# A retention and Fourier-mixing kernel on one core: every engine's queue behind the first batch put in an order that the program text computes

## The chip, the cores and the metric

The kernel runs on one core of a Trainium2 chip. A core has five engines, each with an instruction queue of its own that is worked off in order: TensorE (PE, matrix products; its weight loads are a second row, PEld), VectorE (DVE), ScalarE (ACT), GpSimd (POOL) and SyncE (SP), which here issues DMAs. Engines wait for one another by semaphores. The metric is the device time of one execution in microseconds (us), lower being better. The span is the part of it between the first and the last profiled instruction.

## What is computed

For 4 batches, 8 heads, 768 positions and 64 columns a head, a decaying state is run over the positions; the output (4 x 768 x 512) goes through a two-dimensional Fourier transform of which the real part is added, then through a normalization and two dense layers:

```python
gamma = 1.0 - 2.0 ** (-5.0 - np.arange(H))
for t in range(S):
    state = gamma[None, :, None, None] * state + np.einsum('bhd,bhe->bhde', k[:, :, t], v[:, :, t])
    y[:, :, t] = scale * np.einsum('bhd,bhde->bhe', q[:, :, t], state)
...
X = np.fft.fft(np.fft.fft(x, axis=1), axis=2)
u = x + np.real(X)
un = (u - mu) / np.sqrt(var + 1e-06)
return u + np.maximum(un @ w_ch1, 0.0) @ w_ch2
```

## The kernel before

**Stages of a batch.** Positions are cut into six chunks of 128. Heads are taken in four pairs. For a pair, q, k and v are loaded (`load_unit`, L159, three DMAs of 384 KB on SP's queue into tiles `in32`, 11 buffers), cast to half precision on POOL (`cast_unit`, L355: q16z, kd, v16) and q and k transposed (`t_unit`, L536: on PE with copies on ACT for batches 0 and 1, by DMA transposes on SP's queue for batches 2 and 3). Then come the products within a chunk (`a_unit`, wkA, masked by DVE into atm), the states (`kv_unit`, wkK, chained on DVE through s), and the outputs (`y_unit`, wkY, scaled by ACT into x). DVE folds x by the symmetries of the transform (`fold_s`, `fold_d`, `fold_e`), PE multiplies by cosine and sine tables along the positions (`s1_unit`) and along the columns (`s2_unit`, pq). There DVE makes u, POOL adds x to it (L864, L866), DVE takes mean and variance (bst, L883), and ACT writes the centred un (L885). `unT_unit` transposes un, by PE in batch 0 and half of batch 1, else by a DMA on SP's queue (L910). The dense layers follow for two halves of a batch: `h_unit` (`h0_unit` in the first half of batch 0) makes psh, which ACT or DVE turns into ht (L934, L936, or L954, L956), and `ch_unit` sums psc over 16 blocks of ht (L973), which DVE turns into ob (L977) for a store on SP's queue (L981).

**What runs over what.** The dense layers of batch b are PE's long work. Between their units the program puts the mixing of batch b's second half, and the loads, attention and first mixing of batch b+1. `emit` (L1086) does it: each stream of units gets a start and an end in units of a batch, its units are spread evenly between, and all are written in the order of these times. `dm`, `ts` and `da` (L1122 to L1142) are the starts and ends.

**What sets the order.** The program is written in that order, and the framework then orders each engine's queue with a cost model of its own, earlier text first among what it believes ready. The kernel holds this back in some places by edges that carry no semaphore. `pin` (L98) chains the instructions of the first batch's attention (`first_units`) on each engine, and later on those of POOL for all units with a time below 1.0; `behind` (L113) keeps the units below 1.0 behind the first batch; `held` (L121) and `issue_after` keep casts in turn and the eight maskp instructions (L232) behind one of ACT's. Loads also wait, with semaphores, for a weight load and a matmul (batch 1) or for a matmul of the batch before (batches 2 and 3): L161 and L166.

PSUM tiles, which PE writes and ACT or DVE frees, are of two tags: `g` with five buffers (pq, wkA, wkK, tq, most wkY) and `pm` with three (psh, psc, and the wkY of batch 0).

Of the kernel before, what the change touches and what calls it, by code (L numbers as in the profile page):

```python
# [11 lines left out]
AF = mybir.ActivationFunctionType  # L12
# [18 lines left out]
ON_ACT = {'q': (0, 1, 0), 'kv': (1, 1, 1), 'g': (0, 1, 1), 'gr': (0, 0, 0)}  # L31
FB = 1
NPE = 2
ACT_ROWS = ((2, 5, 6, 7, 8, 9, 10, 14), (0, 3, 6, 7, 9, 10, 11, 12, 14, 15), (2, 4, 5, 6, 7, 8, 10, 14))


@with_exitstack
def kernel(
# [55 lines left out]

    tails, base = {}, {}
    mark = [0]

    def pin(engines=None):  # L98
        ins = tc.nc.cur_bb.bb.instructions
        for n in range(mark[0], len(ins)):  # L100
            x = ins[n]
            e = str(x.engine)
            if engines is not None and not any(g in e for g in engines):
                continue
            if e in tails:
                tc.add_manual_dep(x, tails[e],
                                  mybir.DependencyInfo(mybir.DependencyClass.NoSync,
                                                       mybir.DependencyReason.DATA),
                                  reason="pinned order")
            tails[e] = x.name  # L110
        mark[0] = len(ins)

    def behind():  # L113
        for x in tc.nc.cur_bb.bb.instructions[mark[0]:]:
            if str(x.engine) in base:
                tc.add_manual_dep(x, base[str(x.engine)],
                                  mybir.DependencyInfo(mybir.DependencyClass.NoSync,
                                                       mybir.DependencyReason.DATA),
                                  reason="behind the first batch")

    def held(unit):  # L121
        def run():
            ins = tc.nc.cur_bb.bb.instructions
            n0 = len(ins)
            unit()
            for n in range(n0, len(ins)):
                m = n - 1
                while m >= 0 and ins[m].engine != ins[n].engine:
                    m -= 1
                if m >= 0:  # L130
                    tc.add_manual_dep(ins[n], ins[m].name,
                                      mybir.DependencyInfo(mybir.DependencyClass.NoSync,
                                                           mybir.DependencyReason.DATA),
                                      reason="casts in turn")
        return run


# [14 lines left out]
    def load_unit(b, i, after=None):  # L152
        def run():
            h0 = 2 * PAIR_ORDER[i]
            for name, src in srcs.items():
                t = inp.tile([P, 2, NCH, D], f32, tag="in32", name=f"{name}32")
                rows = "h (p c) d -> p h c d" if b < NPE and name == "q" else \
                    "h (c p) d -> p h c d"
                dma = nc.sync.dma_start(t, src[b, h0:h0 + 2].rearrange(rows, p=P))  # L159
                if after is not None:  # L160
                    for x in (w_dma[after].ins, lb[0]["mm"].ins):  # L161
                        tc.add_manual_dep(dma.ins, x.name,
                                          mybir.DependencyInfo(mybir.DependencyClass.Sync,
                                                               mybir.DependencyReason.DATA),
                                          reason="loads in turn")
                if b > 1:  # L166
                    tc.add_manual_dep(dma.ins, a_of[b - 1, 1].ins.name,
                                      mybir.DependencyInfo(mybir.DependencyClass.Sync,
                                                           mybir.DependencyReason.DATA),
                                      reason="loads behind the transposes")  # L170
                in_of[name, b, i] = t
        return run
# [56 lines left out]
    def late_consts():  # L229
        with tc.issue_after(lb[0]["una"].ins):  # L230
            for h in range(H):
                nc.scalar.activation(maskp[:, h // 2, h % 2], maskf, AF.Copy, bias=0.0,  # L232
                                     scale=float(gam[h] ** (-P)))

# [117 lines left out]

    at, q16_of, kd_of, v16_of, last_cast = {}, {}, {}, {}, {}

    def cast_unit(b, i):  # L355
        def run():
# [3 lines left out]
            v16 = vp.tile([P, NCH, 2, D], f16, tag="v16", name="v16")  # L360
            with ExitStack() as es:
                if b < NPE:
                    if (b, i - 1) in last_cast:
                        es.enter_context(tc.issue_after(last_cast[b, i - 1].ins))
                    q16 = qzs[i % 2].rearrange("p h c d -> p (h c d)")[
                        :, 0:NCH * P].rearrange("p (c h d) -> p c h d", c=NCH, h=2)
                    es.enter_context(tc.issue_after(nc.gpsimd.tensor_scalar(
                        out=q16, in0=q32.rearrange("p h c d -> p c h d"), scalar1=1.0,
                        scalar2=1.0, op0=ALU.mult, op1=ALU.mult).ins))
                else:  # L370
                    q16 = qzs[i % 2]
                    for h2 in range(2):
                        dst = q16[:, h2, :, D * h2:D * h2 + D]
                        nc.gpsimd.tensor_scalar(out=dst, in0=q32[:, h2], scalar1=1.0,
                                                scalar2=1.0, op0=ALU.mult, op1=ALU.mult)
                for h2 in range(2):
                    kc = nc.gpsimd.tensor_scalar(out=kd[:, :, h2, :], in0=k32[:, h2],  # L377
                                                 scalar1=gkd[:, h0 + h2:h0 + h2 + 1],
                                                 scalar2=1.0, op0=ALU.mult, op1=ALU.mult)
                    if b < NPE:  # L380
                        es.enter_context(tc.issue_after(kc.ins))
                last_cast[b, i] = nc.gpsimd.tensor_scalar(  # L382
                    out=v16, in0=v32.rearrange("p h c d -> p c h d"), scalar1=1.0, scalar2=1.0,
                    op0=ALU.mult, op1=ALU.mult)
            q16_of[b, i], kd_of[b, i], v16_of[b, i] = q16, kd, v16
# [26 lines left out]
    def v0_unit(i):  # L412
        def run():
            v32 = in_of.pop(("v", 0, i)).rearrange("p h c d -> p c h d")
            v16 = v16_of[0, i] = vp.tile([P, NCH, 2, D], f16, tag="v16", name="v16")
            n = NCH if i < 3 else 3
            last_cast[0, i] = nc.gpsimd.tensor_scalar(
                out=v16[:, 0:n], in0=v32[:, 0:n], scalar1=1.0, scalar2=1.0, op0=ALU.mult,
# [581 lines left out]
    def attn_steps(b):  # L1000
        steps = []
        for step in range(6):
            un = []
            if step < 4:
                un.append(held(cast_unit(b, step)))
            i = step - 1
# [79 lines left out]
    def emit(streams):  # L1086
# [5 lines left out]
        for e in ev:  # L1092
            e[3]()
            if e[0] < 1.0:
                behind()
                pin(None if e[0] < 0.05 else ["Pool", "GpSimd"])

    pin()
    for u in first_units():
        u()  # L1100
        pin()
    base.update(tails)
    first.close()
# [3 lines left out]
    for b in range(B):  # L1107
# [13 lines left out]
        s2s, unTs = mix_units(b, [3, 4, 5])  # L1121
        dm = (0.12, 0.24, 0.3, 0.38) if b == 0 else (0.004, 0.140, 0.232, 0.341)  # L1122
        streams += [(majors, b, b + 1.0), (s2s, b + dm[0], b + dm[1]),
                    (unTs, b + dm[2], b + dm[3])]
        if b + 1 < B:
            steps = attn_steps(b + 1)
            if b == 0:
                streams.append(([load_unit(1, i, 6) for i in range(4)], 0.180, 0.220))
                streams.append(([qt_zeros], 0.1, 0.15))
                streams.append(([half_tables], 0.655, 0.655 + 0.02))  # L1130
                streams.append(([pad_unit], 0.673, 0.703))
                ts = (0.249, 0.368, 0.410, 0.415, 0.507, 0.615, 0.680, 0.685)
            else:
                streams.append(([load_unit(b + 1, i) for i in range(4)], b + -0.370, b + 0.075))
                n = [len(u) for u in steps[1:]]
                ts = [-0.040, -0.020] + [0.050 + 0.585 * sum(n[:j]) / sum(n)
                                         for j in range(6)]
            streams.append((steps[0], b + ts[0], b + ts[1]))
            streams += [(u, b + ts[j + 2], b + ts[j + 3]) for j, u in enumerate(steps[1:])]
            end = b + ts[-1]  # L1140
            da = (0.062, 0.080, 0.173, 0.203, 0.271, 0.321) if b == 0 else \
                (0.063, 0.067, 0.048, 0.158, 0.168, 0.189)  # L1142
            streams.append(([s1_unit(b + 1, e, cb) for cb in range(2) for e in range(2)
                             if cb or b + 1 >= FB], end + da[0], end + da[1]))
            s2s, unTs = mix_units(b + 1, [0, 1, 2])
            streams += [(s2s, end + da[2], end + da[3]), (unTs, end + da[4], end + da[5])]
    emit(streams)


# [28 lines left out]
```

## Time and profile before

| | |
|---|---|
| median of 4 runs | 247.71 us (247.35 to 247.93) |
| the profiled execution | 247.35 us |
| its span | 245.4 us |
| matmuls, and other instructions busy | 2024; DVE 430, ACT 276, POOL 146 |
| dense layers, psc at L973 | 400 matmuls, busy 89.6 us |
| dense layers, psh at L930 | 448 matmuls, busy 81.3 us |
| moved by DMA | 36.39 MB, mean 148 GB/s |

A row of the profile's groups names the line, the engine, the operation, the tiles (out<-in), the shapes and the count, then the busy time, the mean of one and the idle time of its engine just before it with what ended that. The chain that ended last is followed backwards from the last instruction, at each step to what released it. In the 40 slices a digit is the busy share in tenths. "issue" is time in which an engine waited for nothing that the profile shows.

### The profile page before, as it was taken

How to read it: one execution, taken by the hardware profiler on the slowest of the kernel's cores; microseconds unless marked ns; L12 is line 12 of the kernel's file. 1: busy time of each engine (PE TensorE's matmuls, PEld its weight loads, DVE VectorE, ACT ScalarE, POOL GpSimd, SP SyncE). 2: the span in 40 equal slices, each digit the busy share in tenths (PEclk: the TensorE clock that was granted, in tenths of full speed). 3: DMA queues.
4: the chain of work that ended last, by engine and by line, in shares of the span. 5: the costliest groups of instructions: out<-in, count | busy, mean ns of one | idle time of the engine just before them, and what ended most of it. 6: DMA issues, size and time to landing. Idle time of an engine off the chain costs nothing.

```text
span 245.4 us, 5309 instructions
## 1 busy us (share of the span) xinstructions
PE 233.5 (95%) x2024; PEld 144.1 (59%) x2024; DVE 177.7 (72%) x430; ACT 124.1 (51%) x276; POOL 81.0 (33%) x146
## 2 busy tenths in 40 slices
PE   6797899999999999999999999999999998999994
PEld 2454668856776655665567446665676455445543
DVE  8999957899788788995986648887885657324112
ACT  8798678487786445742247416722357217202500
POOL 7667500494500068680001637650003214000000
DMA  8999999899999188989999489596100331121012
GB/s 177 259 258 145 202 198 198 185 250 265 279 218 227 26 171 189 196 165 148 262 277 203 97 177 188 103 137 161 47 0 3 63 130 33 35 85 43 0 45 85
DMA packets 99209, 36.39 MB, mean 148 GB/s; under 512 B 89840, under 2 KB 96240, under 8 KB 99184
## 3 DMA queue, kind: packets, MB, share of 16 engines
q1 hardware_dynamic: 94960, 31.86, 62.9%
q0 software_dynamic: 4224, 4.19, 10.7%
q8 instruction: 16, 0.26, 0.5%
q14 instruction: 9, 0.07, 0.1%
HBM read 27.26 MB, written 6.29 MB: 137 GB/s over the span
## 4 chain that ended last, share of the span: by engine, by line
PE 71%; DVE 9%; POOL 6%; ACT 5%; SPq 3%; DMA 2%; issue 2%; POOLq 0%; DVEq 0%
PE psc L973 30%; PE psh L930 23%; PE ps L730 3%; SPq L159 3%; PE psh L947 3%; PE wkA L594 3%; DMA k<-in_k_dram 2%; PE wkY L648 2%; DVE bst L883 2%; POOL u L866 2%; PE wkY L644 1%; POOL u L864 1%; PE wkK L613 1%; DVE u L834 1%; PE pq L827 1%
## 5 line engine op out<-in xcount | busy, mean ns | idle before, releaser
L973 PE MATMUL psc<-w,ht 128*128 128x512 f16 (+1 forms) x400 | 89.6, 370 | 0.1
L930 PE MATMUL psh<-unT,w 128*128 128x384 f16 x448 | 81.3, 326 | 0.6 <-ACT ht L934 0.6
L973 PEld LDWEIGHTS <-ht 128*128 128x128 f16 x400 | 38.1, 98 | 35.5 <-issue 0.3
L930 PEld LDWEIGHTS <-w 128*128 128x128 f16 x448 | 42.3, 98 | 24.9 <-issue 1.3
L934 ACT ACTIVATE ht<-psh 128x384 f16<-128x384 f32 x64 | 30.6, 488 | 39.4 <-PE psh L930 38.2
L864 POOL TENSOR_TENSOR u<-u,x 128x256 f32<-128x256 f32 x21 | 13.3, 635 | 102.6 <-DVE u L834 91.0
L977 DVE SCALAR_TENSOR_TENSOR ob<-psc,stats,u 128x512 f32<-128x512 f32 (+1 forms) x25 | 18.1, 722 | 27.1 <-PE psc L973 27.0
L936 DVE TENSOR_SCALAR ht<-psh 128x384 f16<-128x384 f32 x48 | 26.3, 549 | 8.6 <-PE psh L930 8.3
L597 DVE TENSOR_TENSOR atm<-wkA,maskp 128x512 f16<-128x512 f32 x36 | 23.9, 683 | 1.0 <-PE wkA L594 1.0
L885 ACT ACTIVATE un<-u,stats 128x512 f16<-128x512 f32 x21 | 15.1, 721 | 16.9 <-DVE stats L884 8.7
L883 DVE BATCH_NORM_STATS2 bst<-u 128x6 f32<-128x512 f32 x21 | 14.6, 694 | 9.8 <-POOL u L866 9.5
L623 DVE SCALAR_TENSOR_TENSOR s<-s,gk,wkK 128x128 f16<-128x128 f16 x48 | 16.4, 342 | 2.3 <-ACT s L619 1.4
L656 ACT ACTIVATE x<-wkY,gexp 128x384 f16<-128x384 f32 x24 | 12.8, 580 | 9.3 <-PE wkY L648 9.3
L145 PE MATMUL wps<-ht 128*128 128x512 f16 x40 | 12.6, 418 | 2.2 <-POOL ht L196 2.2
L377 POOL TENSOR_SCALAR kd<-k,gexp 128x384 f16<-128x384 f32 x24 | 13.9, 587 | 1.9 <-DMA k<-in_k_dram 1.9
L866 POOL TENSOR_TENSOR u<-u,x 128x256 f32<-128x256 f32 x21 | 13.3, 635 | 2.8 <-DVE u L858 1.3
L594 PE MATMUL wkA<-qTz,kT 128*128 128x256 f16 x72 | 13.6, 273 | 0.0
L829 ACT COPY qn<-pq 128x128 f32<-128x128 f32 x18 | 4.9, 274 | 14.1 <-PE pq L827 13.9
L947 PE MATMUL psh<-unT,w 128*128 128x128 f16 x192 | 11.5, 219 | 0.1
L947 PEld LDWEIGHTS <-w 128*128 128x128 f16 x192 | 11.0, 98 | 0.7 <-issue 0.5
L382 POOL TENSOR_SCALAR v<-v 128x768 f16<-128x768 f32 x12 | 10.0, 830 | 2.2 <-DMA v<-in_v_dram 2.1
L594 PEld LDWEIGHTS <-kT 128*128 128x128 f16 x72 | 6.9, 98 | 6.0 <-DVE s L623 0.4
(164 smaller groups left out, 317.3 us busy)
## 6 DMA issues: line engine op xcount, KB each, us to landing
q<-in_q_dram SPq DMA_DIRECT2D x16, 384.0 KB, 6.1
k<-in_k_dram SPq DMA_DIRECT2D x16, 384.0 KB, 5.6
v<-in_v_dram SPq DMA_DIRECT2D x16, 384.0 KB, 6.5
out_dram<-ob SPq DMA_DIRECT2D x23, 256.0 KB, 2.6
w<-in_moe_w_ch_dram POOLq DMA_DIRECT2D x8, 512.0 KB, 10.8
out_dram<-ob SPq DMA_DIRECT2D x2, 128.0 KB, 1.7
unT<-un SPq DMA_TRANSPOSE x15, 2.4
qTz<-q16z SPq DMA_TRANSPOSE x8, 3.8
```

What stands on the lines that cost most here:

```text
L594: mm = nc.tensor.matmul(wk[:, c2], st["kT"][:, c, :], st["qT"][:, :, c, :], start=True, stop=True)
L597: nc.vector.tensor_tensor(out=st["atm"][:, 2 * part:2 * part + 2], in0=wk, in1=maskp[:, PAIR_ORDER[i]].unsqueeze(1).to_broadcast([P, 2, 2, ...
L623: nc.vector.scalar_tensor_tensor(out=s16[:, c], in0=s16[:, c - 1], scalar=gk2[:, hp:hp + 1], in1=wk[:, c - c0], op0=ALU.mult, op1=ALU.add)
L864: nc.gpsimd.tensor_tensor(out=u[:, kb, 0:256], in0=u[:, kb, 0:256], in1=x[:, kb, 0, 1:257], op=ALU.add)
L866: nc.gpsimd.tensor_tensor(out=u[:, kb, 256:512], in0=u[:, kb, 256:512], in1=x[:, kb, 1, 257:1:-1], op=ALU.add)
L883: nc.vector.bn_stats(bst, u[:, kb, :])
L930: nc.tensor.matmul(psh, w116[:, cb, fb * P:(fb + 1) * P], unT[:, cb, rt * 384:(rt + 1) * 384], start=(cb == 0), stop=(cb == 3))
L934: nc.scalar.activation(ht16[:, fb, :], psh, AF.Relu, bias=0.0, scale=-1.0)
L936: nc.vector.tensor_scalar(out=ht16[:, fb, :], in0=psh, scalar1=-1.0, scalar2=0.0, op0=ALU.mult, op1=ALU.max)
L947: mm = nc.tensor.matmul(psh[:, f], w116[:, cb, fb * P:(fb + 1) * P], unT[:, cb, kb * P:(kb + 1) * P], start=(cb == 0), stop=(cb == 3))
L973: nc.tensor.matmul(psc[:, c0:c1], ht16[:, fb, rb3 * P:(rb3 + 1) * P], w216[:, fb, c0:c1], start=(fb == 0), stop=(fb == NFB - 1))
L977: nc.vector.scalar_tensor_tensor(out=ob[:, c0:c1], in0=psc[:, c0:c1], scalar=lb[b]["st"][:, rb, 3:4], in1=lb[b]["u"][:, rb, c0:c1], op0=AL ...
```

## The change

The helpers `pin`, `behind`, `held` and the uses of `issue_after` go. `emit` only writes units in the order of their times. All instructions written up to the end of `first_units` are counted as `kept`. At the end the new `order_queues` looks at every instruction, works out what each needs (tiles read and written, buffers of a ring, PSUM banks, the `told` semaphore edges of the loads), gives each a due time, plays the program through with durations from `instr_cost`, and chains each engine's instructions, SP's among them, in the order that results. Those in `kept` stay in program order.

A due time is worked out backwards. A PE instruction is due at the sum of the PE durations before it in the program. Any other is due 12 us after the PE time at its place in the program, or earlier, where something that needs it is due earlier, less its own duration and a lag. In the play-through each engine takes, among what is ready, what is due first. DMAs of SP share one ring (`dma`), POOL's another (`soft`).

```diff
+SLACK = 12000.0
+BY_DUE = ('PE', 'DVE', 'Activation', 'Pool', 'SP')
+def instr_cost(x, PSUM=PSUM):
...
+    if eng == "PE":
+        return max(n / 2.4 + 2.5, 27.0) * (0.5 if half else 1.0), n / 2.4 + 165.0
+    if kind == "InstDMACopy":
+        return (780.0 if eng == "Pool" else 400.0), None
+    if kind == "InstDmaTransposeAnt":
+        return 1400.0, 3800.0 if el > 600 else 2450.0
...
+            t = 100.0 + el * (1.04 if wide or not x.ins else 0.45)
+        return t, t + 80.0
+    if eng == "Activation":
+        t = 65.0 + 0.83 * el + (80.0 if scaled else 0.0) + (0.0 if psum else 90.0)
+        return t, t + 105.0
+    two = kind == "InstTensorTensor"
+    t = 80.0 + 2.3 * el if two else (250.0 + 0.7 * el if el > 300 else 80.0 + 1.0 * el)
+    return t, t + 30.0
+def order_queues(tc, told, kept):
...
+    for n in range(kept):
+        if eng[n] in last:
+            need[n][last[eng[n]]] = 0
+        last[eng[n]] = n
...
+    lag = {"DVE": 35.0, "Activation": 36.0, "Pool": 78.0, "PE": 79.0, "SP": 26.0}
...
+        due[n] = now + (0.0 if eng[n] == "PE" else SLACK)
+        if eng[n] == "PE":
+            now += spans[n][0]
+    for n in sorted(range(len(ins)), key=lambda n: -n):
+        for m, k in then[n]:
+            gap = 0.0 if not k or eng[n] == eng[m] == "PE" else lag[eng[m]] + (
+                spans[n][1] or 6000.0)
+            due[n] = min(due[n], due[m] - gap)
...
+        n = heapq.heappop(ready[e])[1]
+        order[e].append(n)
+        free[e] = t + busy
+        if span is None or e == "SP":
...
+                if not there:
+                    big = size > 600 * 128
+                    end = max(t + (3100.0 if big else 2500.0),
+                              dma + (1450.0 if big else 900.0))
+                    free[e] = max(t + 1220.0, end - 2400.0)
+                else:
+                    run = list(there[0].ap)[-1][1] * 4
+                    work = 4.0 * size / (217.0 if run <= 256 else 345.0)
+                    put = any(x is there[0] for x in list(ins[n].outs))
+                    end = max(t + 1500.0 + work + (0.0 if put else 700.0), dma + work)
+                    free[e] = max(t + (330.0 if put else 450.0),
+                                  end - (3000.0 if put else 4550.0))
+                dma = end
...
+    for v in order.values():
+        for a, b in zip(v, v[1:]):
+            tc.add_manual_dep(ins[b], ins[a].name,
+                              mybir.DependencyInfo(mybir.DependencyClass.NoSync,
+                                                   mybir.DependencyReason.DATA),
+                              reason="order of the queue")
...
-            if e[0] < 1.0:
-                behind()
-                pin(None if e[0] < 0.05 else ["Pool", "GpSimd"])
...
-        dm = (0.12, 0.24, 0.3, 0.38) if b == 0 else (0.004, 0.140, 0.232, 0.341)
+        dm = DM0 if b == 0 else DM1
...
     emit(streams)
+    order_queues(tc, told, kept)
```

The starts and ends become constants at the top of the file, and some have new values:

```diff
+DM0, DM1 = (0.120, 0.245, 0.307, 0.391), (0.054, 0.205, 0.240, 0.286)
+TS0 = (0.249, 0.336, 0.337, 0.405, 0.476, 0.584, 0.649, 0.654)
-                ts = (0.249, 0.368, 0.410, 0.415, 0.507, 0.615, 0.680, 0.685)
+TS1 = (-0.040, -0.020, 0.050, 0.585)
+DA0, DA1 = (0.069, 0.096, 0.179, 0.265, 0.276, 0.326), (0.063, 0.067, 0.048, 0.158, 0.168, 0.189)
-            da = (0.062, 0.080, 0.173, 0.203, 0.271, 0.321) if b == 0 else \
-                (0.063, 0.067, 0.048, 0.158, 0.168, 0.189)
+LD0, LD1 = (0.180, 0.220), (-0.370, 0.094)
-                streams.append(([load_unit(b + 1, i) for i in range(4)], b + -0.370, b + 0.075))
+HT0 = (0.655, 0.712, 0.673, 0.708)
-                streams.append(([half_tables], 0.655, 0.655 + 0.02))
-                streams.append(([pad_unit], 0.673, 0.703))
```

TS1, LD0 and DA1 hold the old values. No arithmetic and no shape of an instruction changes, and no instruction is added or taken away.

## The prediction

> **What bounds the kernel now.** I read the page first, its busy shares and its 40 slices.
>
> ```profile
> span 245.4 us, 5309 instructions
> PE 233.5 (95%) x2024; PEld 144.1 (59%) x2024; DVE 177.7 (72%) x430; ACT 124.1 (51%) x276; POOL 81.0 (33%) x146
> ...
> PE   6797899999999999999999999999999998999994
> ```
>
> TensorE (PE) is busy in nearly every slice after the sixth. So this isn't a kernel in which a queue order can uncover much: what it can give back is PE's own stops. The busy table by stage, then, to see where they are (columns: stretch, its length, busy time and instructions of PE, PEld, DVE, ACT, POOL, granted clock, DMA share, GB/s):
>
> ```profile
> 34.30:41.00 6.70, 6.43 (x93) 5.45 (x91) 4.20 (x12) 6.09 (x21) 0.26 (x4) 1.00 1.22 193
> ...
> 90.00:96.00 6.00, 5.48 (x45) 3.20 (x44) 4.85 (x13) 3.25 (x9) 4.64 (x9) 1.00 0.81 170
> 96.00:150.00 54.00, 54.00 (x428) 32.88 (x426) 41.51 (x98) 22.99 (x53) 19.32 (x33) 1.00 1.01 188
> 150.00:158.00 8.00, 7.60 (x74) 5.06 (x72) 7.09 (x18) 5.62 (x15) 6.15 (x12) 1.00 0.74 171
> ...
> 199.00:211.00 12.00, 11.28 (x76) 6.81 (x75) 9.27 (x22) 6.83 (x18) 3.68 (x6) 1.00 0.17 45
> ```
>
> The reader sees that the clock is full everywhere, and that PE's losses sit in a few short stretches (90 to 96, 150 to 158, 199 to 211). Over 34.3 to 242.3 us, which is what the change orders anew, these rows and the others of the table add up to 2.2 us of idle PE.
>
> That is too little by the end of each pipe: a lone 512-column matmul shows 379 ns, while 48 in a row take 10.36 us, 216 ns each, so every stop hides 163 ns more. I therefore took, in the trace, every distance from one matmul's start to the next one's and subtracted the usual step of its shape (216 ns for 512 columns, 162 for 384, 109 for 256, 56 for 128). From 34.2 us to the last matmul 202.1 us are such steps and **5.6 us** are excess. Eighteen stops of over 80 ns hold 4.9 of it. No order can gain more than 5.6, since the steps themselves stay.
>
> Here the Trainium skill ("Perfetto Trace Analysis", Identifying the Most-Contended Engine) warns that busy matmuls say little about headroom and that weight-load time is the better measure. The row for that is 59%, which read as headroom would be 41% of the span, 100 us. I go by the steps: one load here serves 384 or 512 streamed columns, so 59% cannot grow to 100 by reordering.
>
> **Which work stops PE.** Three pieces of the chain that ended last, for the largest stops:
>
> ```profile
> 90.98 0.62 POOL u L866
> 91.59 0.96 POOL q16z L374 x2
> 92.55 1.13 POOL kd L377 x2
> 93.68 0.81 POOL v L382
> 94.53 0.44 PE wkK L613 x5
> ```
>
> Batch 2's first casts stand behind the additions to u, though their loads had landed by 73.5 us (issued 64.9 to 66.3); PE waits at the wkK matmuls. The two stops there cost 0.84 us of excess, the twin at 155.8 to 156.7 (wkY waiting for DVE's u and atm) 0.73.
>
> ```profile
> 203.74 0.72 ACT L885 ACTIVATE un<-u,stats 128x512 f16<-128x512 f32 x1 [0.60 <-DVE stats L884]
> 204.37 1.23 ACT L934 ACTIVATE ht<-psh 128x384 f16<-128x384 f32 x3
> ...
> 206.29 0.72 ACT L885 ACTIVATE un<-u,stats 128x512 f16<-128x512 f32 x1 [0.36 <-issue]
> 206.92 0.85 ACT L934 ACTIVATE ht<-psh 128x384 f16<-128x384 f32 x2
> ```
>
> In the last batch ACT takes un, which feeds matmuls at 221.4, ahead of ht, for which PE already stands. The three stops from 204.4 to 210.6 are 0.365 + 0.600 + 0.240 = 1.21 us.
>
> ```profile
> 38.34 1.69 ACT L232 ACTIVATE maskp<-maskf 128x128 f32<-128x128 f32 x8
> 39.94 1.05 ACT L954 ACTIVATE ht<-psh 128x512 f16<-128x512 f32 x2
> ```
>
> ACT makes maskp (first used by atm at 57.7 us), and DVE clears qTz (two memsets of 378 ns), before the ht that frees PE's buffer: 0.28 us.
>
> **The change part by part.** *Removed*: the pins, `behind`, `held`, `issue_after`. They are edges without semaphores; no instruction goes, so 0. *Added*: one edge between each pair of neighbours on each queue, again no instruction and no semaphore, 0; the same 5309 instructions run. Should an edge make one more wait per stop, the nearest row is the 0.02 to 0.07 us of "issue" in the chain; over 18 stops 0.4 to 1.3 us, my upper bound on the loss; below, 0. I take 0. *The first batch* (`kept`) stays in order, so 0 to 34.3 us is unchanged, and so is the end: after the last matmul at 242.2 only ob (0.48) and its store follow.
>
> *The order itself.* An instruction of another engine is now due when the matmul that needs it is due, less its time. Un due at 221 goes behind ht due in a microsecond; maskp and the memsets, used over 12 us later, go behind ht; the casts run in POOL's own gap of 20 us before 86.7. So I take as gone the three big groups, 0.84 + 0.73 + 1.21 = 2.78, and 0.28 at 40.2: **3.06 us**. Cover of the moved work: un then has 211 to 221.4, where ACT and DVE are busy 0.00 and 1.95 of 10.40; without that cover it costs its old price, 1.2. POOL, once early with the casts, must still not be late with u, which stops nothing today but bst.
>
> I take as not gained the stops where the engines are full or the data late: 0.39 at 58 to 59 (two ACT copies of 0.79 and one of 0.80 in a row; DVE is at 16.4 of 19.0 from 41 to 60), 0.25 at 75 to 77 behind atm, 0.32 at 80.8 behind xg, 0.18 at 127 and 180, 0.65 at 34 to 38 behind the first batch's chain, and 0.8 in small ones. Were they all gone too, the gain would be 5.6; that is the low end.
>
> *What the model misjudges comes back as new stops*, since the order is fixed. Its cast of 384 elements takes 250 + 0.7 x 384 = 519 ns against 585 for kd, of 768 elements 788 against 831, its atm 632 against 681. Per pair of heads 2 x 66 + 43 + 3 x 49 = 0.32 us, for 12 pairs 3.9 us if nothing hides it, 0 if PE always has other work. PE had none for 5.6 of 208 us, so I lean to the low side and take 0.5 us (an estimate). *The new constants* (DM1 moves s2 of batches 1 to 3 from 0.004..0.140 to 0.054..0.205 of a batch, TS0 the casts of batch 1 from 0.368 to 0.336) change program order, hence the due times, those of the s2 by 0.05 to 0.065 of the 52 us between two batches, 2.6 to 3.4 us; the unT that they lead to are needed at half a batch, 26 us in. I take 0, as they move inside that; if the cover were gone, the price is the old one of such a stop, 0.6.
>
> *The SP queue* now carries loads, stores and transposes by due time. Each load holds the ring for 1.66 us (batch 1's twelve land between 47.46 and 65.75 us, 1.1 to 2.3 apart). The transposes must land before wkA: the cover from the later landing of a pair's two to its first wkA is 2.4, 0.6, 1.5, 2.1 us in batch 2 and 2.1, 2.9, 0.6, 3.6 in batch 3. So one load put ahead of every pair costs 1.06 + 0.16 + 1.06 = 2.3, none costs 0. Behind a transpose that waits on SP stand the next loads and the stores; ob has three buffers, so DVE's ob and then psc on PE would be late next. I take 0: the model bills ring time for loads (98,304 x 4 / 217 = 1.81 us) close to these rows, and today's order already puts a load of 6.6 us ahead of a transpose of 6.5 us without a stop. The Trainium skill ("DMA: Bandwidth & Descriptors", Anatomy of one DMA) has 2.0 us plus bytes over 436 GB/s for a transfer that GpSimd issues, which makes, as an estimate, 2.9 us for 384 KB and 0.9 of ring; the rows of this case's SP loads say 5.6 to 6.5 to landing. By the page a load ahead of every pair would cost only 0.3 + 0.3 = 0.6, and a model that bills twice its ring time would hold back transposes for nothing.
>
> **Sum**: 3.06 - 0.5 = 2.5 us. The profiled execution took 247.35 (span 245.4 and 1.95 around it); it was the fastest of four with median 247.71. 247.7 - 2.5 = **245.2**.
>
> **Rivals.** *Everything gained* (0.15): all stops but the first batch's 0.65 go, 5.0 less 0.3: 243.0. For it: every stop has work behind it that could go first. Against: DVE is at 7.09 of 8.00 from 150 to 158. *Moved, not removed* (0.10): PE, freed at 94 and 156, stands at the next fixed head; the 3.9 us of misjudged casts come in at three quarters and the sum is 0: 247.7. For it: stops with "issue" or atm as their end follow where PE runs ahead; against: misses of 0.05 us each are shorter than any stop counted. *Slower: transposes behind loads* (0.18). If due times put two loads (3.3 us) ahead of a pair, it overshoots its cover by 0.9, 2.7, 1.8, 1.2, 1.2, 0.4, 2.7, 0, mean 1.36; in three pairs of eight that is 4.1, less the 2.5 gained: 249.3. It decides from two pairs on. For it: batch 3's loads go out amid batch 2's transposes (96 to 118 us), both on SP. Against: the covers held with mixed orders so far. If the edges changed nothing in the order at all, the time would be 247.7, within the second rival.
>
> **Numbers.** Forecast 0.57, of gains between 1 and 4 us: its own range 243.6 to 246.8. Four runs differ by 0.58 us, so 0.2%, 0.5 us, is about what can be told from none. Faster 0.57 + 0.15 = 0.72, same 0.10, slower 0.18. The range leaves about 0.07 below and 0.13 above: 242.7 to 248.6.
>
> **What would show it.** The stages 90 to 96, 150 to 158 and 199 to 211 (a little earlier then) with PE idle under 0.2 each; maskp on ACT well after 41 us; un of batch 3 after the last ht of its half; casts of batch 2 in the seventies or early eighties. POOL's wait for u is no measure. Wrong would be PE waits of over 0.5 us at wkA or wkK with a DMA or cast as releaser (the slower rival), or many new stops of 0.1 to 0.3 that sum to 3 us (the second).

## The result, and the profile after

| | before | after |
|---|---|---|
| median | 247.66 us (247.22 to 247.97, 61 runs) | 247.62 us (246.66 to 248.70, 38 runs) |
| ratio after to before | | 1.0002, 95% interval 0.9996 to 1.0008 |
| profiled execution, span | 247.35, 245.4 us | 248.68, 246.6 us |
| matmul steps from 34.2 us on | 202.1 us | 202.2 us |
| excess over the steps | 5.64 us | 6.79 us |

The change made no difference; 245.2 had been forecast. The profiled execution of after is at the upper end of its runs, which spread over 2.0 us where those of before spread over 0.75. It is 1.1 us slower than the median, so its excess may be more than that of a middling execution. The page of after:

```profile
span 246.6 us, 5286 instructions
...
PE 233.2 (95%) x2024; PEld 144.2 (58%) x2024; DVE 178.7 (72%) x430; ACT 123.7 (50%) x276; POOL 82.5 (33%) x146
...
PE 65%; DMA 9%; ACT 7%; DVE 7%; SPq 5%; POOL 3%; issue 2%; ACTq 0%; POOLq 0%; DVEq 0%
```

The same matmuls and nearly the same busy time. The prediction had the same 5309 instructions run; it is 5286, by 23 waits on semaphores fewer in the trace, while the 4900 that keep an engine busy and the DMAs are the same. But the chain that ended last, 71% PE and 2% DMA before, now runs through DMAs for 9% of the span. By stage (columns: stretch, length, busy time of PE, PEld, DVE, ACT, POOL, granted clock, DMA share, GB/s):

```profile
34.30:41.00 6.70, 6.05 (x90) 5.51 (x89) 3.55 (x12) 6.03 (x19) 0.26 (x4) 1.00 1.23 199
41.00:47.00 6.00, 5.37 (x91) 5.00 (x89) 5.80 (x14) 3.49 (x11) 3.69 (x6) 1.00 0.62 108
55.00:66.00 11.00, 10.03 (x99) 6.25 (x98) 6.87 (x17) 6.06 (x10) 6.05 (x9) 1.00 1.25 261
...
90.00:96.00 6.00, 6.00 (x41) 3.15 (x40) 4.85 (x12) 2.87 (x7) 5.76 (x11) 1.00 1.06 229
96.00:150.00 54.00, 53.57 (x426) 32.41 (x424) 42.30 (x100) 23.09 (x56) 21.91 (x36) 1.00 0.98 182
150.00:158.00 8.00, 8.00 (x68) 5.47 (x66) 6.18 (x14) 4.77 (x15) 2.90 (x5) 1.00 0.74 168
158.00:165.00 7.00, 6.22 (x59) 3.90 (x58) 6.63 (x16) 2.60 (x7) 2.71 (x5) 1.00 0.47 92
199.00:211.00 12.00, 12.00 (x80) 7.16 (x79) 6.66 (x13) 4.44 (x13) 2.45 (x4) 1.00 0.12 44
```

The stages 90 to 96, 150 to 158 and 199 to 211 have no idle PE any more: the three big stops are gone. In their place are new ones: 41 to 47 (full before) and 55 to 66 (10.94 before) together lack 1.6 us, 158 to 165 lacks 0.8 and the stretch before 150 lacks 0.4. Two pieces of the chain lead to the last two:

```profile
130.00 5.37 DMA q<-in_q_dram
...
136.81 0.51 POOL q16z L569
137.32 0.60 POOL u L1057
...
141.34 3.78 DMA unT<-un
145.14 0.04 ACTq L1078
145.18 0.05 issue
145.22 0.72 ACT un L1078
145.95 0.20 ACT stats L1094
...
148.31 6.64 DMA v<-in_v_dram
...
155.13 0.80 POOL v L576
155.93 1.13 POOL kd L573 x2
157.06 0.60 POOL u L1057
```

Twice POOL's fixed queue has an addition to u behind a cast whose load is still on its way. And at 141.34 the transpose of un takes 3.8 us, because one load of batch 3 went out on SP just ahead; ACT's third un waits for it (un has two buffers), and behind that un stands the square root (of the variance) that ob needs.

### The profile page after: what moved, and what is told of

Read it like the earlier page. It is cut to its first block, busy times and chain, and to the rows that moved or that the text cites. A ratio compares the mean times of both kernels' runs of the same rounds, so it can differ in the third digit from the quotient of the medians.

```text
span 246.6 us, 5286 instructions
## 1 busy us (share of the span) xinstructions
PE 233.2 (95%) x2024; PEld 144.2 (58%) x2024; DVE 178.7 (72%) x430; ACT 123.7 (50%) x276; POOL 82.5 (33%) x146
## 4 chain that ended last, share of the span: by engine, by line
PE 65%; DMA 9%; ACT 7%; DVE 7%; SPq 5%; POOL 3%; issue 2%; ACTq 0%; POOLq 0%; DVEq 0%
PE psc L1166 29%; PE psh L1123 21%; SPq L358 4%; PE ps L923 3%; DMA v<-in_v_dram 3%; PE wkA L787 2%; DMA k<-in_k_dram 2%; DMA q<-in_q_dram 2%; DMA unT<-un 2%; PE wkY L841 2%; PE psh L1140 2%; PE wkY L837 1%; DVE xab L866 1%; PE pq L1020 1%; ACT qTz L749 1%
## 5 line engine op out<-in xcount | busy, mean ns | idle before, releaser
L1127 ACT ACTIVATE ht<-psh 128x384 f16<-128x384 f32 x64 | 31.1, 491 | 50.5 <-PE psh L1123 49.7
L573 POOL TENSOR_SCALAR kd<-k,gexp 128x384 f16<-128x384 f32 x24 | 15.0, 634 | 9.4 <-DMA k<-in_k_dram 7.9
L787 PE MATMUL wkA<-qTz,kT 128*128 128x256 f16 x72 | 13.1, 272 | 1.0 <-ACT qTz L749 0.4
L569 POOL TENSOR_SCALAR q16z<-q 128x384 f16<-128x384 f32 x16 | 8.0, 516 | 15.5 <-DMA q<-in_q_dram 12.8
L1027 DVE SCALAR_TENSOR_TENSOR u<-pq,g,qn 128x256 f32<-128x256 f32 x18 | 8.6, 480 | 4.0 <-PE psh L1123 2.3
```

The source lines that it names most:

```text
L787: mm = nc.tensor.matmul(wk[:, c2], st["kT"][:, c, :], st["qT"][:, :, c, :], start=True, stop=True)
L1127: nc.scalar.activation(ht16[:, fb, :], psh, AF.Relu, bias=0.0, scale=-1.0)
```

## The experiments

All kernels were timed against the kernel before. The expectations letter their theories and say what each means; in those of e8 and e10 "u of the second half of batch 2" should read the first half, row blocks 0 to 2. "Excess" is, as in the prediction, what matmuls' distances exceed the usual step by, from 34.2 us on.

### Does the order or do the constants make the difference?

The old constants in the changed kernel (all, `DM1` alone, all but `DM1`), and the new constants in the kernel before:

```diff
-DM0, DM1 = (0.120, 0.245, 0.307, 0.391), (0.054, 0.205, 0.240, 0.286)
-TS0 = (0.249, 0.336, 0.337, 0.405, 0.476, 0.584, 0.649, 0.654)
+DM0, DM1 = (0.12, 0.24, 0.3, 0.38), (0.004, 0.140, 0.232, 0.341)
+TS0 = (0.249, 0.368, 0.410, 0.415, 0.507, 0.615, 0.680, 0.685)
...
```

> The changed kernel with the starts and ends of before (DM0, DM1, TS0, DA0, LD1, HT0), so the new ordering alone. Theory A: the weight load is still mis-sized, so 247 to 249. Theory B: the time falls to about 245. Theory C: about 247.6.

> The changed kernel with one constant of before, DM1 (when s2 and unT of batches 1 to 3 are written), ring rate 205. With all constants of before it took 259.8, with long stops near 95 and 155 us, in the first halves of batches 2 and 3. If DM1 makes these, 256 to 260; if the attention's times (TS0, DA0, LD1) do, 247 to 250.

> The counterpart: the changed kernel with DM0, TS0, DA0, LD1 and HT0 of before and the new DM1, ring rate 205. If the attention's times and loads make the long stops, 254 to 260; if DM1 makes them, 247 to 250.

> The kernel before with the changed kernel's starts and ends, its own pins and the framework's order: the constants alone. Theory B: slower than before by 1 to 3 us (248.5 to 250.5). Theories A and C: within 1 us of before (246.7 to 248.7), since the constants were not what moved the stops.

| | old order | new order |
|---|---|---|
| old constants | 247.66 | e2: 259.75, ratio 1.0479 [1.0453, 1.0506] |
| old `DM1`, rest new | | e6: 253.71, 1.0242 [1.0210, 1.0273] |
| new `DM1`, rest old | | e7: 253.18, 1.0243 [1.0209, 1.0277] |
| new constants | e3: 254.37, 1.0277 [1.0264, 1.0290] | 247.62 |

None of the ranges expected for these four held. The constants aren't small: they cost the old order 6.7 us and are worth 12.1 to the new one, about 6 for each group. Nor does either part bring a gain alone. In e2 and e6 the largest stop is at the same place, ahead of the dense layers of batch 2 (e2: 5.8 us at 155.0, e6: 4.5 at 148.6), and PE then runs at half speed for some microseconds. Stages of e2:

```profile
155.00:161.00 6.00, 0.34 (x5) 0.14 (x3) 2.44 (x6) 1.74 (x7) 2.44 (x4) 0.86 0.57 67
161.00:167.00 6.00, 6.00 (x22) 2.86 (x22) 2.88 (x9) 0.49 (x1) 1.39 (x3) 0.57 0.29 112
```

PE stands for nearly all of 155 to 161, and in the next six, though busy, it gets 22 matmuls done at a granted clock of 0.57: a 384-column step took 320 ns in place of 162.

### The weight loads' price

The model bills a weight load on GpSimd's ring 262,144 x 4 / 205 bytes per ns = 5.1 us. The eight landed at 25.73, 29.45, 31.99, 34.56, 37.33, 39.99, 42.63 and 45.21 us, and in the kernel before likewise, 2.5 to 2.9 us apart behind the second. Batch 1's loads wait for the seventh and a matmul. With its prices and the trace's first issue, 20.2, the model has the seventh in at 20.2 + 1.9 + 7 x 5.1 + 0.6 = some 58.4 us, while the first load went out at 45.27: it orders 34 to 70 us for operands that come 13 us earlier than it thinks.

```diff
-                soft = max(soft, t + 1900.0) + 4.0 * size / 205.0
+                soft = max(soft, t + 1900.0) + 4.0 * size / 396.0
```

> One number of the changed kernel's play-through is altered: the rate of GpSimd's DMA ring from 205 to 396 bytes per ns. The text bills a weight load 262,144 x 4 / 205 = 5.1 us of ring; the eight of the changed kernel land about 2.65 us apart. So it expects batch 1's first load after the seventh weight load at 20.2 + 1.9 + 7 x 5.1 + 0.6 = 58.5 us, where it was issued at 45.3, and orders everything from 34 to 72 us for operands 13 us later than they come. Theory A (this mis-sized load made the new stops between 34 and 70 us): the stops there, 0.79 + 1.12 + 1.9 us in the changed kernel, fall to under 1, and the time to 244 to 245 (ratio to before 0.985 to 0.990). Theory B (the new starts and ends give back what the order gains) and theory C (any fixed order makes as many new stops as it removes, by small misjudgements of casts and masks): no change beyond 0.3 percent, 247 to 248.

246.93 us (246.37 to 247.51), ratio 0.9976 [0.9966, 0.9986]: a little faster than both kernels, but not theory A's 244 to 245, and the stops between 34 and 70 us still sum to 2.1 us, where it had under 1. Those from 41 to 47 are gone, those of 61 to 69 too, and others came; the excess is 5.06. The first of these stages in e1:

```profile
41.00:47.00 6.00, 6.00 (x106) 5.94 (x104) 5.07 (x12) 3.91 (x11) 1.30 (x3) 1.00 0.88 180
```

With the old constants as well:

> Both: the ring rate at 396 and the starts and ends of before. Theory A: 244 to 246, the ordering gains with either set of constants. Theory B: below the run with the rate alone by 1 us or more. Theory C: about 247.6.

250.77 us, ratio 1.0128 [1.0101, 1.0155], slower than all three theories had it: the price is worth 9 of the 12 us that the old constants cost, but the new ones still are 3.8 better. One of its stops, 1.68 us at 148.3, is at the same place.

### A table load that the model doesn't have

Of e1's stops, 0.84 and 0.51 us lie at 57 to 59. ACT's timeline there:

```profile
55.13 1.28 ACT L1094 ACT_TABLE_LOAD   x1
56.43 0.30 ACT L1094 ACTIVATE stats<-stats,epsT 128x3 f32<-128x3 f32 x1
56.63 1.59 ACT L749 COPY qTz<-tq 64x768 f16<-64x768 f16 x2
58.26 0.30 ACT L1094 ACTIVATE stats<-stats,epsT 128x3 f32<-128x3 f32 x1
```

The first root brings its function table in, 1.283 us that no price covers, and the second root stands ahead of kT, for which PE waits. Billing it:

```diff
...
+    table = next(n for n, x in enumerate(ins) if x.name == told_table[0])
+    spans[table] = tuple(c + 1283.0 for c in spans[table])
...
```

> On top of the ring rate of 396, the play-through also learns of the one load of ACT's function table, 1.283 us before the first square root (L1094), which it bills nothing. In the run with the ring rate alone PE stands 0.84 and 0.50 us at 57.3 and 58.7 behind ACT's qTz and kT, which that load pushes back. Theory A (the new stops come from work that the play-through doesn't know of): those two go, 1.3 us less, 245.4 to 246. Theory C (any fixed order makes as many new stops): another stop appears in their place, 246.5 to 247.5.

246.18 us (245.89 to 246.51), ratio 0.9944 [0.9932, 0.9956], just above theory A's range; of the two stops, 1.34 us, 0.37 are left. On ACT the second root now goes behind kT and unT, and 56 to 62 has 5.95 us of PE busy where e1 has 4.98:

```profile
56.88 1.59 ACT L751 COPY qTz<-tq 64x768 f16<-64x768 f16 x2
58.50 0.80 ACT L756 COPY kT<-tq 128x768 f16<-128x768 f16 x1
59.19 0.59 ACT L1117 COPY unT<-pst 128x512 f16<-128x512 f16 x1
59.67 0.31 ACT L1096 ACTIVATE stats<-stats,epsT 128x3 f32<-128x3 f32 x1
```

### A dearer price for DVE's folds

The largest stop left in e4, 1.55 us at 78.0, waits for DVE's xg behind the folds, of which one took 853 ns beside a cast on POOL (12 folds of before: 548 to 567). So folds of over 600 elements were billed 0.62 ns an element in place of 0.45.

> As the run before, and DVE's operations of over 600 half-precision elements (the folds) billed 100 + 0.62 x 768 = 576 ns in place of 446; with the ring rate alone these took 464 to 470 ns from start to start by themselves, but 853 where POOL casts at the same time, and PE stood 1.56 us at 78.8 behind them. Theory A: that stop shrinks to under 0.8, 244.5 to 245.5. Theory C: no less than the run with the table load.

248.78 us, ratio 1.0056 [1.0036, 1.0075]. The fold's stop fell only to 1.01, and one of 2.10 us came at 146.2. Theory A, that each better price gives its own stops back, falls here; theory C had it. The chain of e5 into that new stop:

```profile
140.19 4.95 DMA unT<-un
...
145.25 0.72 ACT un L1080
145.97 0.20 ACT stats L1096
...
146.33 0.61 issue
146.94 0.75 DVE ob L1173
```

### Additions to u behind casts

The loads behind the first batch billed as landing 2.5 or 1.5 us later, on e4's kernel, so that POOL takes u ahead of casts that wait for loads:

```diff
+                    late = 0.0 if put or n < kept else 2500.0
...
+                end += 0.0 if not there else late
```

> The kernel of e4_table_load with one more billing: the loads behind the first batch count as landing 2.5 us later than the model says, so the program places the additions to u (POOL) of the second half of batch 2 ahead of the casts that wait for batch 3's loads. Theory D (what is left over the steps is the head of POOL's queue: additions to u behind a cast that waits for a load): the stop at 146.7 goes (0.24 us), no new one over 0.3 comes between 130 and 165, the executions lie closer together than those of e4 (0.6 us) and the time is 245.4 to 246.2. Theory C (every change of a price shuffles the rest, and what goes in one place comes back in another): 246.2 to 249, with a new stop of over 0.5 us elsewhere.

> As e8_late_loads_2500, with 1.5 us in place of 2.5, so that only some of the additions to u go ahead of the casts. Theory D: between e4_table_load and e8_late_loads_2500, 245.6 to 246.3. Theory C: no relation to the size of the billing; it may be slower than both by over 1 us.

245.98 us, ratio 0.9934 [0.9921, 0.9948], and 246.44, 0.9952 [0.9940, 0.9965]. Neither can be told from e4. Theory D has the time of e8, but not its sign that no new stop comes, and e9 is just outside its range. In e8 all six additions came from 133.3 to 137.6 as wanted (136.2 to 140.4 in e4), and no stop came from 150 on, but one of 1.85 us at 145.1. SP's queue of e8 there (start, time on the queue, what), and the ACT instruction that waits:

```profile
137.45 0.57 SPq L362 DMA_DIRECT2D q<-in_q_dram  x1
138.08 0.95 SPq L362 DMA_DIRECT2D k<-in_k_dram  x1
139.13 6.74 SPq L1108 DMA_TRANSPOSE unT<-un  x3
```
```profile
143.93 0.72 ACT L1082 ACTIVATE un<-u,stats 128x512 f16<-128x512 f32 x1 [5.56 <-DMA unT<-un]
144.56 0.29 ACT L1098 ACTIVATE stats<-stats,epsT 128x3 f32<-128x3 f32 x1
```

In the kernel before, the nearest load stood 4.5 us ahead of the same transposes, and the first of them landed 2.48 us after its issue (4.70 in e8):

```profile
132.78 1.30 SPq L159 DMA_DIRECT2D k<-in_k_dram  x1
137.26 3.61 SPq L910 DMA_TRANSPOSE unT<-un  x2
```

e8's is e5's chain: two loads of batch 3, ready a few tenths earlier, went out ahead of the three transposes, and un, root and ob came late one after another. The model couldn't see un's wait, for it makes a new tile wait only for the users of the old one that stand earlier in the program text; wherever the third un is written ahead of the first transpose, that wait is missing (7 of the 8 half batches, counted in the text).

### The transposes ahead of the loads

Two things were put right: the missing wait, and the place of one load, by an edge set by hand. Both on e8's kernel and on e4's; each alone on e8's; both on the changed kernel itself:

```diff
...
+    for ring, bufs in sizes.values():
+        for old, new in zip(ring, ring[bufs:]):
+            for m in users[old]:
+                need[users[new][0]][m] = 1
...
+    for late, early in behind:
+        need[at[late]][at[early]] = 0
...
+    behind = [(ld_of[3, i, w], tr_of[2, kb]) for i, w, kb in ((3, "q", 2),)]
...
```

> The kernel of e8_late_loads_2500 with two things more in the model: the third un of a half waits for the transpose of the first (un has two buffers, and the model leaves this wait out wherever the transpose stands later in the program text), and the q load of batch 3's fourth pair goes on SP's queue behind the three transposes of batch 2's first half, not ahead of them. Theory F (the stop of 1.85 us at 145.1 comes from two loads of 1.7 us each ahead of the transposes on SP: un, and behind it on ACT the root for ob, wait for the first of them): that stop goes, ACT's wait for unT falls from 5.6 to under 3 us, and the time is 245.98 - 1.85 = 244.1, within 243.9 to 244.7. Theory C (what goes in one place comes back in another): 245.5 to 247, with a new stop of over 0.8 us between 140 and 165 for the casts whose loads now go later.

> The same two things on the kernel of e4_table_load, so without the 2.5 us on the loads: the additions to u still stand behind casts. Theory F with D: the gain is no more than e4's stop there, 0.24 us, so 245.9 to 246.3, and the stops at 78 and 95 stay as in e4. Theory C: anywhere from 245.5 to 248.

> One half of e10_transposes_ahead: the model knows that the third un waits for the first transpose, but the q and k loads stay ahead of the transposes on SP. Theory G (the missing wait in the model is what costs, since the root for ob stood behind a waiting un on ACT): the stop of 1.85 goes and the time is 244.2 to 244.7. Theory H (the loads ahead of the transposes cost): psh still stands for the third unT, a stop of 0.6 to 1.8 stays between 144 and 148, 245.0 to 246.2.

> The other half: the q load (and with it the k load) goes behind the three transposes, and the model still leaves out the wait of the third un. Theory G: the root stays behind the waiting un, but un waits less, so a stop of 0.3 to 1.8 stays: 244.6 to 246. Theory H: no stop over 0.2 between 140 and 150, 244.1 to 244.6.

> The changed kernel itself (weights still billed at 205, no load of the table, loads not late) with the two things of e10_transposes_ahead. If the four causes act one by one, only the stop at 147.7 (0.50 us) goes: 247.62 - 0.5 = 247.1, within 246.6 to 247.5. If the wrong wait alone spoils the order, as theory G has it in the strong form, 245 to 246. Theory C: 247 to 249.

| | us | ratio to before | excess |
|---|---|---|---|
| e8 | 245.98 | 0.9934 [0.9921, 0.9948] | 4.18 |
| e12: e8 and the wait | 248.57 | 1.0045 [1.0020, 1.0071] | 7.28 |
| e13: e8 and the load behind | 244.59 | 0.9877 [0.9864, 0.9890] | 2.44 |
| e10: e8 and both | **244.26** (244.22 to 244.32) | **0.9860 [0.9848, 0.9873]** | 2.35 |
| e11: e4 and both | 245.90 (245.28 to 247.74) | 0.9929 [0.9904, 0.9954] | 3.93 |
| e14: after and both | 247.14 (246.75 to 247.27) | 0.9970 [0.9959, 0.9982] | 5.14 |

The place of the load makes the stop: with the load behind (e13) no stop over 0.2 is left between 140 and 150, as theory H has it. e10, e11 and e14 came within the first range given for each. e12 came out as neither G nor H said: knowing the wait without moving the load is worse than e8. Both loads still go out ahead, since the model takes the next thing that is ready and can't hold a load back for a transpose that will be ready a little later. The third transpose now goes out behind a further load and stores, and lands at 149.46 (147.10 in e8), with psh waiting for it. SP's queue of e12:

```profile
143.92 0.42 SPq L368 DMA_DIRECT2D v<-in_v_dram  x1
...
145.32 1.46 SPq L1114 DMA_TRANSPOSE unT<-un  x1
```

SP's queue and ACT in e10:

```profile
137.61 2.50 SPq L1118 DMA_TRANSPOSE unT<-un  x2
140.20 0.53 SPq L1190 DMA_DIRECT2D out_dram<-ob  x1
141.16 1.19 SPq L1118 DMA_TRANSPOSE unT<-un  x1
142.41 0.57 SPq L371 DMA_DIRECT2D q<-in_q_dram  x1
```
```profile
138.58 0.30 ACT L1108 ACTIVATE stats<-stats,epsT 128x3 f32<-128x3 f32 x1 [0.20 <-DVE stats L1091]
140.41 0.72 ACT L1092 ACTIVATE un<-u,stats 128x512 f16<-128x512 f32 x1 [1.53 <-DMA unT<-un]
```

The load goes out five microseconds later, and no stop of PE over 0.1 comes behind it; the root stands ahead of the waiting un. In e14 the stop at 147.7 is gone, and so are those at 160 to 161 (158 to 165 has 7.00 of 7.00): POOL's last casts there ended at 154.6 and the additions to u followed at once, where after had them from 157.0. Whether the load's place or the rest of the new order did that isn't separated; e4, with the load ahead, has no stop there either.

All fifteen kernels with the new order can be sorted by the number of batch 3's loads that stand on SP's queue directly ahead of the first of those three transposes:

| loads ahead | PE's stop there, us |
|---|---|
| 0 | e10, e11, e13, e14: none |
| 1 | after 0.50, e1 0.48, e4 0.24, e7 none, e9 none |
| 2 | e1b 1.68, e5 2.10, e8 1.85, e12 2.43 in two |
| 3 | e6 4.46, e2 5.82 |

"None" is nothing over 0.1. In e2 the chain names POOL's cast of the third of these loads, but un reads nothing of that cast; the first transpose landed at 157.51 and un began 0.10 us later, as it did in e8 (143.83 and 143.93). One load does not always make a stop: in e7 and e9 the transposes came in time. What looked like theory C, gains that come back anywhere, was in e1b, e5, e8 and e12 and in the largest stops of e2 and e6 this one place. e7 has none there, and its largest stops (2.2 and 1.5 us at 95 to 100, ahead of PE's transposes of un) were not followed further.

## Why the prediction was wrong

**What bounds the kernel: right.** PE's steps stayed at some 202 us in every run, and the differences were excess. The edges can't cost much: e10 has one between all neighbours on all queues, and 2.35 us of excess in all, of which six stops hold 1.9.

**The stops named: right but for the last.** 2.78 us at 93 to 94, 156 and 204 to 211 went. The 0.28 at 40 did not turn into a gain: the eight maskp were to come well after 41 us, and seven still stood in front. ACT in after:

```profile
40.34 1.53 ACT L432 ACTIVATE maskp<-maskf 128x128 f32<-128x128 f32 x7
41.75 0.65 ACT L1048 COPY qn<-pq 128x255 f32<-128x255 f32 x2
42.27 0.64 ACT L1147 ACTIVATE ht<-psh 128x512 f16<-128x512 f32 x1
```

Casts of batch 2 did move into the seventies and eighties (POOL busy 4.65 us from 75 to 85, 0.00 before), and un of batch 3 behind its ht.

**The step that failed: "What the model misjudges comes back as new stops", taken at 0.5 us.** It measured 3.0: with no new stops the forecast's sum makes 247.7 - 3.06 = 244.6, and after took 247.62. e10 took 244.26; in it two prices and a wait are put right, loads are billed late, and one load is held behind by hand. That it lies so near 244.6 is partly luck: it has 0.93 us behind the folds where before had 0.32, but the 0.39 at 58 to 59 and the 0.25 at 75 to 77, not counted as gains, are gone. The parts of these 3.36 us from after to e10, each on top of the ones before: weight loads 0.69 (e1), table load 0.75 (e4), loads billed later 0.20 (e8, not to be told from nothing), a load no longer ahead of unT 1.39 (e13), the missing wait 0.33 (e10, hardly to be told from e13). They don't simply add. On the changed kernel by itself the last two give 0.48 (e14). And e11 and e10, which differ by the late billing alone, are 1.64 us apart: e8's 0.20 is two things, for e4's stops at 58 to 60, 78, 95 and 128 shrink by some 1.6 while the one at the transposes grows from 0.24 to 1.85, which e13 takes back. Whether the loads do land later than the model says was not compared. The step looked for misjudged work where the durations are easy to compare, in casts and atm, a few hundredths each; no stop was traced to those. What cost was billed wrong by microseconds (a weight load 5.1 for 2.6) or left out (a table load, a wait for a buffer). Nor does any price cover that folds and casts stretch each other, up to 1171 ns for the 446 billed; the 0.93 us that e10 still has stand behind two such folds. The trace of before had the weight loads' landings; the check of the ring's price was made for SP's loads alone.

**The constants: wrong at 0.** They were costed against the old order, where the cover of unT was half a batch. They suit the new one, with its wrong prices: 12.1 us there. Which of them does what was not followed further, and the model of e10 was not run with the old ones.

**The SP queue: wrong at 0.** The slower rival had the mechanism, transposes behind loads, but looked for it at qTz and kT with covers of 0.6 to 3.6 us and from two pairs on. It came at unT, where the same step found "half a batch" and no queue. On the changed kernel it cost 0.5 us, not enough to make it slower.

**"POOL must still not be late with u, which stops nothing today but bst"** named the second place and priced it at nothing. In after, u behind the v cast of 155.1 leads to 1.1 us of stops at 160 and 161, which e14 doesn't have.

The rival "moved, not removed" had the time, 247.7, by luck: the cause was another than its 0.32 us a pair.

## What to carry over

A fixed order computed from prices is only as good as its worst price: before relying on one, compare its billed time with the trace for each kind of work, the rare ones first (eight weight loads, one table load), and check that every wait the program has, a buffer's reuse included, is in it. Even a better price or a wait put right can give a worse order (e5, e12). A play-through that takes whatever is ready next can't hold back a transfer for a more urgent one that is ready a few tenths later, so look on a shared DMA queue at what stands directly ahead of each transfer that something waits for. When constants and an order are tuned together, neither can be judged alone.

## What the runs showed of the hardware

PE's clock can fall to half behind short stops. In e12 two of 0.75 and 1.36 us, within 2.5 us, were enough (columns as in the stages above):

```profile
150.00:154.00 4.00, 3.42 (x14) 1.54 (x12) 2.35 (x5) 0.49 (x1) 1.75 (x3) 0.57 0.00 0
154.00:158.00 4.00, 4.00 (x26) 2.43 (x25) 2.04 (x6) 2.33 (x5) 0.00 (x0) 1.00 0.00 1
```

The Trainium skill ("TensorE: Matmul & The Clock Gate", Part 1: The HAM clock gate) has the clock fall after at least one idle window of about 3.4 us; here PE was at work for part of any such window, and the measurement decides. The steps at half speed that followed cost a further 1.1 us. It doesn't come every time: five of e12's twelve executions have a mean clock of 0.993 and took 249.4 to 250.9 us, the other seven 247.3 to 248.6; in e5 it was three of six.

DVE's folds (two half-precision inputs, 768 elements) took 545 to 568 ns alone and up to 1171 ns in e10, where casts run beside them, and a cast of 384 elements 941 in place of 510 in e1. The Trainium skill ("SBUF — State Buffer", SBUF: two separate sides) has DVE instructions with two inputs from SBUF and GpSimd ones that read SBUF lock each other out of a shared pair of ports, which fits these times. Behind the first batch the order of before never let them meet: its 16 casts of that kind all took 510 to 512.
